# Two token rows and one mirrored block turned by DMA instead of TensorE, in a spectral filter with a gated MLP

## The chip, the core and the metric

The kernel runs on one core of a Trainium2 chip. The metric is the device time of one execution in microseconds (us). A core has a matrix engine (TensorE, PE in the profile; its weight loads are PEld), a vector engine (VectorE, DVE), a scalar engine (ScalarE, ACT), GpSimd (POOL), a queue engine (SyncE, SP), and 16 DMA engines that carry what the queues of SP and ACT issue. [...]

## What is computed

`x` is a 2048 x 512 array in bf16 (2048 tokens). It is normalised per token, and two branches are added to it: a filter in the two-dimensional Fourier domain, and a gated MLP with 1792 hidden columns.

```
xn = layernorm(x)                                   # per token, over 512
X  = rfft2(xn) * (w_r + 1j * w_i)
y  = irfft2(X)                                      # spectral branch
h  = gelu(xn @ w_gate, tanh form) * (xn @ w_up)     # 512 -> 1792
out = x + y + h @ w_down                            # 1792 -> 512
```

## The kernel before

**Tiles.** The tokens form 16 rows of 128 (a row here is 128 tokens on the 128 partitions), four rows to a block. The hidden columns form 14 groups of 128 (`NFC`). For every row the kernel loads `x`, takes mean and variance (`stats`, L519), a reciprocal root (`root_act` L523 for rows 0 and 1, `root_pool` L529 on GpSimd for the others), normalises (`norm`, L535) into `xn`, and turns the 128 x 512 row into `xnT` with features on the partitions. Both branches read `xnT`.

**Turning a row.** There are three ways. `first_half` (L557) turns row 0 in two halves on PE. `turn` (L540) does a row with four PE transposes into PSUM (L550) and one VectorE copy to `xnT` (L555); rows 1, 2 and 3 go this way. `turn_dma` (L577) has SP issue one DMA transpose from SBUF to SBUF; rows 4 to 15 go this way. `mirror(b)` (L589) makes, for each block, one more 128 x 512 tile from the normalised rows (a difference of reversed parts, one VectorE operation) and turns that too: by PE and a VectorE copy (L604, L608) for block 0, by a DMA transpose (L595) for blocks 1 to 3. `fold(b)` (L610) combines `xnT` and the turned mirror tile on VectorE and feeds the first Fourier matmuls (L635, evicted by ScalarE at L640).

**The spectral branch** after that is a long chain of VectorE operations (`tt`, recorded at L467), with small matmuls (L850, L931, L991) and ScalarE evictions between, and ends in additions to `x`, four rows at a time.

**The MLP.** `gated` (L709) does one group for a stretch of tokens: four gate matmuls and four up matmuls (L718) over the four feature parts; each four are a burst, and each burst writes one of three PSUM banks; ScalarE applies gelu to the gate (L723) and copies the up part (L724), VectorE multiplies them into `hT` (L725). A block is 512 tokens wide. Block 0 begins before all its rows are there: `first` (L728) does groups 0 to 2 for rows 0 and 1, row by row; then groups 3 to `NHALF`-1 are done for rows 0 and 1 (256 tokens, first halves); then all groups below `NHALF` for rows 2 and 3 (second halves); then the groups from `NHALF` on for all 512 tokens. Blocks 1 to 3 follow in full width. `down` (L756) sums 14 matmuls (L766) with `wd` for one row; the rows of block b are placed between the groups of block b+1. For the last block, `down` uses PSUM slots of the spectral branch, and VectorE adds straight from PSUM (L777); for the others ScalarE copies (L774) and VectorE adds (L775).

**Loads.** The gate and up weights come in column slabs 0:384 (groups 0 to 2, on ACT's queue), 384:768 (groups 3 to 5), 768:1280 (groups 6 to 9) and 1280:1792 (groups 10 to 13). SP issues, in order: rows 0 to 3 one by one, the slabs 384:768, rows 4 to 7, the slabs 768:1280, rows 8 to 11, the slabs 1280:1792, the Fourier tables (`small`), rows 12 to 15. Each of these is one DMA with a semaphore of its own. `wd` is issued after row 7 is normalised, the table `tf` after row 11, the filter after the last fold.

**The order of work** is set before the program is written out, by a planner (`_Sched`, L145). It simulates the engines with a cost for each operation (for a DMA: bytes at a fixed rate in one queue, plus a lag) and always takes the operation that can start first; among those of the same engine within 0.05 us it takes the one with the smallest key (its ready time plus an offset `key`) or, where one is given, its due time. The result is a fixed order on each engine, with semaphore waits. MLP matmuls carry large, rising keys: they fill PE in their own order wherever no other PE operation is ready. `STAT` and `NORM` are due times: row s (4 and up) has its statistics due at STAT[0] + STAT[1] * (s - 4), its normalisation at NORM[0] + NORM[1] * (s - 4). `gate` is a list of operations after which SP may issue loads that are declared later.

```
filler = []
for fc in range(NFIRST, NHALF):
    filler.append(("g", 0, fc, 0, 256))
for fc in range(NHALF):
    filler.append(("g", 0, fc, 256, 256))
for fc in range(NHALF, NFC):
    filler.append(("g", 0, fc, 0, 512))
```

Of the kernel before, what the change touches and what calls it, by code (L numbers as in the profile page):

```python
# [14 lines left out]
FF = 1792  # L15
P = 128
NFC = 14
NHALF = 6
NFIRST = 3
WARM = 10 * (512,) + (256,)  # L20
HKEY = 1.5
NORM = 15.0, 1.5
STAT = 13.0, 1.2
SLACK = 0.05
MARGIN = 1.0
RATE = 340e3
# [118 lines left out]
class _Sched:  # L145
# [11 lines left out]
    def op(self, eng, cost, fn, reads=(), writes=(), tiles=(), key=0.0, after=(), dma=0, lag=0.0, due=None, land=None):  # L157
        o = _Op()
        o.eng, o.fn, o.cost, o.key, o.dma, o.lag, o.due, o.land = eng, fn, cost, key, dma, lag, due, land
        o.reads, o.writes, o.tiles = reads, writes, [(t, False) for t in tiles]  # L160
        o.extra = [a for a in after if a is not None]
        o.seq = len(self.ops)
        o.end = None
        o.pos = None
        self.ops.append(o)
        return o
# [184 lines left out]
def bass_parallel_sum__spectral_gfnet__glu_gated_geglu__prompt_kernel(  # L351
# [11 lines left out]
    c_small = nc.inline_tensor(small_np, name="c_small")  # L363
# [5 lines left out]
    wgv = B_w_gate.rearrange("(dc p) f -> p dc f", p=P)  # L369
    wuv = B_w_up.rearrange("(dc p) f -> p dc f", p=P)  # L370
# [3 lines left out]
    op = sch.op  # L374

    with ExitStack() as es:
        def sb(name, shape, dt=BF16, cell=0):
            n = int(np.prod(shape))
            t = es.enter_context(nc.sbuf_tensor(name, [P, n], dt))
            return view(t, name, 0, shape, cell)  # L380
# [15 lines left out]
        wg = sb("wg", [4, FF])  # L396
        wu = sb("wu", [4, FF])
        wd = sb("wd", [NFC, D])
        small = sb("smallc", [9, P])
# [21 lines left out]
        ident = small[:, 0]  # L421
# [6 lines left out]
        ps_sp_bf = ps_sp[:, :].bitcast(BF16)  # L428
# [30 lines left out]
        gate = []  # L459

        def dma(q, dst, src, nbytes, wr=None, rd=None, key=0.0, after=(), cost=0.41, lag=0.0, land=None):
            after = tuple(after) + tuple(gate if q == "sp" else ())
            return op(q, cost, lambda e: e.dma_start(dst() if callable(dst) else dst.ap, src() if callable(src) else src.ap),
                      reads=rd if rd is not None else (), writes=wr if wr is not None else (), dma=nbytes, key=key, after=after, lag=lag, land=land)

        def tt(o, a, b, f, n, key=0.0, **kw):
            return op("dve", c_tt(n), lambda e: e.tensor_tensor(o.ap, a.ap, b.ap, f), reads=(a, b), writes=(o,), key=key, **kw)  # L467
# [13 lines left out]
        def load(q, dst, src, nbytes, **kw):  # L481
            return dma(q, dst, lambda: src, nbytes, wr=(dst,), **kw)

        def wload(q, dst, src, lo, hi, **kw):
            return load(q, dst[:, :, lo:hi], src[:, :, lo:hi], (hi - lo) * 1024, **kw)

        k = iter(np.arange(0.0, 1.0, 0.001))
        def rows(lo, hi, land=None):
            return load("sp", x[:, lo:hi], xb[:, lo:hi, :], (hi - lo) * 131072, key=next(k), land=land)
# [8 lines left out]
            rows(i, i + 1, 6.3 + 0.3 * i)  # L498
        for w, v in ((wg, wgv), (wu, wuv)):
            wload("sp", w, v, 384, 768, key=next(k))  # L500
        rows(4, 8)
        for w, v in ((wg, wgv), (wu, wuv)):
            wload("sp", w, v, 768, 1280, key=next(k))
        rows(8, 12)
        for w, v in ((wg, wgv), (wu, wuv)):
            wload("sp", w, v, 1280, FF, key=next(k))
        load("sp", small[:, 1:9].rs([8 * P]), c_small.ap()[:, P:], 262144, key=next(k))
        rows(12, 16)
        op("pool", 0.1, lambda e: e.memset(eps.ap, LN_EPS), writes=(eps,), key=-2)
        op("pool", 0.1, lambda e: e.memset(half.ap, -0.5), writes=(half,), key=0)  # L510

# [4 lines left out]
        def xn(s):  # L516
            return RB(8192 + 512 * (s % 8), [4, P])

        def stats(s, key, due=None, after=()):  # L519
            op("dve", 0.61, lambda e: e.bn_stats(bst[:, s].ap, xs(s).ap), reads=(xs(s),), writes=(bst[:, s],), key=key, due=due, after=after)  # L520
            op("dve", 0.11, lambda e: e.bn_aggr(bag[:, s].ap, bst[:, s].ap), reads=(bst[:, s],), writes=(bag[:, s],), key=key, due=due)
# [7 lines left out]
        def root_pool(s0, n, key):  # L529
            sl = slice(s0, s0 + n)  # L530
            v, y, h = vv[:, sl], rs[:, sl], half[:, sl]
            op("pool", 0.2 + 0.03 * n, lambda e: e.tensor_scalar(v.ap, bag.ap[:, sl, 1], LN_EPS, None, ADD), reads=(bag[:, sl],), writes=(v,), key=key)
            op("pool", 0.5 + 0.14 * n, lambda e: e.tensor_tensor(y.ap, v.ap, h.ap, ALU.pow), reads=(v, h), writes=(y,), key=key)

        def norm(s, key, due=None):  # L535
            o, i = xn(s).rs([512]), xs(s)
            op("dve", 0.34, lambda e: e.tensor_scalar(o.ap, i.ap, bag.ap[:, s, 0:1], rs.ap[:, s:s + 1], SUB, MUL),
               reads=(i, bag[:, s], rs[:, s:s + 1]), writes=(o,), key=key, due=due)

        def turn(s0, n, key):  # L540
            b, sl = s0 // 4, s0 % 4
            t = _T("sp")

            def bank():
                return ps_sp_bf[:, t.slot * 2048:t.slot * 2048 + 512 * n]

            def f(e):
                ins = None
                for i in range(4 * n):
                    ins = e.transpose(bank()[:, i * P:(i + 1) * P], xn(s0 + i // 4).ap[:, i % 4], ident.ap)  # L550
                return ins

            o = xnT[:, b, sl:sl + n].rs([512 * n])
            op("pe", 4 * n * 0.056, f, reads=tuple(xn(s0 + i) for i in range(n)) + (ident,), tiles=(t,), key=-40, lag=0.1)
            op("dve", 0.08 + n * 0.26, lambda e: e.tensor_copy(o.ap, bank()), writes=(o,), tiles=(t,), key=key)  # L555
# [20 lines left out]

        def turn_dma(s):  # L577
            i, o = xn(s), xnT[:, s // 4, s % 4]
            op("sp", 1.25, lambda e: e.dma_start_transpose(o.ap, i.rs([512]).ap), reads=(i,), writes=(o,), dma=425000, key=-5.0)


        Y = R1(0, [16, D])
# [4 lines left out]
        odd, turned = {}, {}  # L587

        def mirror(b):  # L589
            rows = RB(8192 + 2048 * (b % 2), [4, 4, P])  # L590
            g = RB(2048 * (b % 2) + 1024, [4, P])
            odd[b] = RB(2048 * (b % 2) + 1536, [4, P])
            tt(g, rows[:, :, 1, ::-1], rows[:, :, 3, ::-1], SUB, 512, 0.5)
            if b:
                op("sp", 1.25, lambda e: e.dma_start_transpose(odd[b].ap, g.rs([512]).ap), reads=(g,), writes=(odd[b],), dma=425000, key=-5.0)  # L595
                return
            t = _T("sp")

            def bank():
                return ps_sp_bf[:, t.slot * 2048:t.slot * 2048 + 512]  # L600

            def f(e):
                for i in range(4):
                    ins = e.transpose(bank()[:, i * P:(i + 1) * P], g.ap[:, i], ident.ap)  # L604
                return ins

            op("pe", 4 * 0.056, f, reads=(g, ident), tiles=(t,), key=2.0, lag=0.1)
            op("dve", 0.34, lambda e: e.tensor_copy(odd[b].rs([512]).ap, bank()), writes=(odd[b],), tiles=(t,), key=1.0)  # L608

        def fold(b):  # L610
            par = b % 2
# [42 lines left out]
        for s in (2, 3):  # L654
            root_pool(s, 1, -50.0)
            norm(s, -50.0)
            early = sch.ops[-1]
            turn(s, 1, -50.0)
        mirror(0)
        fold(0)  # L660
        for s in range(4, 16):
            stats(s, 0.0, STAT[0] + STAT[1] * (s - 4), (early,))
            if s % 2 == 1:
                root_pool(s - 1, 2, -4.0)
        hold = {}
        for s in range(4, 16):
            norm(s, 0.0, NORM[0] + NORM[1] * (s - 4))
            hold[s] = sch.ops[-1]
            turn_dma(s)
            if s % 4 == 3:  # L670
                mirror(s // 4)
                fold(s // 4)
# [113 lines left out]
# [7 lines that stand above are left out]
# [51 lines left out]
        for v, hh in ((4, (12, 13)), (0, (14, 15)), (2, (8, 9)), (6, (10, 11)), (1, (0, 1)), (7, (4, 6)), (3, (2, 7)), (5, (5, 3))):  # L844
            t = _T("sp")
# [17 lines left out]
        for ri, f in ((0, ADD), (1, SUB)):  # L863
            op("pool", 0.3, lambda e, ri=ri, f=f: e.tensor_tensor(edge.ap[:, ri], ev[0].ap[:, ri], ev[1].ap[:, ri], f),
               reads=(ev[0][:, ri], ev[1][:, ri]), writes=(edge[:, ri],), key=1.0)
# [53 lines left out]
        for i, v in enumerate((0, 4, 1, 7, 2, 6, 3, 5)):  # L919
            t = _T("sp")  # L920

            def f_i(e, v=v, t=t):
# [15 lines left out]
               writes=(gv,), tiles=(t,), key=-0.5)  # L938
# [40 lines left out]
        for jq in range(4):  # L979
# [4 lines left out]
            for jp in (2 * jq, 2 * jq + 1):  # L984
                t = _T("sp")
# [57 lines left out]
```

## Time and profile before

| What | us |
|---|---|
| median of 3 runs | 171.29 (171.24 to 171.5) |
| the profiled execution | 171.29 |
| its span, first to last instruction | 169.4 |
| PE busy | 166.3 |
| VectorE busy | 146.0 |
| ScalarE busy | 106.3 |
| the 12 DMA transposes of rows, issue to landing | 2.5 to 8.4, median 4.5 |

Times inside a profile count from the start of its span. A row of the timeline gives start, duration, engine, line, operation, tiles written <- read, shape and count, and in brackets the idle time before it and what ended it; "SPq" and "ACTq" are instructions that issue DMAs. Matmul durations overlap, so PE's pace is read from starts.

### The profile page before, as it was taken

The numbers are of one execution on the slowest core, as the hardware profiler recorded it, in microseconds if no ns is written. First come the engines' busy times: TensorE is split into PE (matmuls) and PEld (weight loads), VectorE is DVE, ScalarE is ACT, GpSimd is POOL, SyncE is SP. The second block draws the span as 40 slices with busy tenths as digits, with TensorE's granted clock in tenths as the row PEclk, the third lists the DMA queues.
The fourth block names the chain that finished last, engine by engine and source line by source line (L and its number), as shares of the span: only waits on it lengthen the run. The fifth ranks groups of instructions, "written<-read, shape, count | busy, mean of one in ns | idle before, by whom it ended". The sixth has DMA issues, their size and how long they took to land.

```text
span 169.4 us, 2695 instructions
## 1 busy us (share of the span) xinstructions
PE 166.3 (98%) x999; PEld 86.1 (51%) x999; DVE 146.0 (86%) x293; ACT 106.3 (63%) x174; POOL 12.3 (7%) x25
## 2 busy tenths in 40 slices
PE   8999999999999999999999999999999999999994
PEld 3698544445555444444444554644445654444443
DVE  2889999995975999999999999999999869963932
ACT  3588766663979739589663695875738896561000
POOL 2032253500000000020000000000000000000000
PEclk9999999999999999999999999999999999999999
DMA  5999999994025262510000000000000003300322
GB/s 146 338 350 347 286 132 300 224 255 101 0 55 127 76 136 79 159 61 0 0 0 0 0 4 0 0 0 0 4 0 2 0 4 106 128 13 0 124 67 62
DMA packets 22239, 15.62 MB, mean 92 GB/s; under 512 B 9293, under 2 KB 21586, under 8 KB 22226
## 3 DMA queue, kind: packets, MB, share of 16 engines
q1 hardware_dynamic: 21026, 14.63, 34.6%
q10 hardware_dynamic: 1200, 0.82, 1.6%
q8 instruction: 8, 0.13, 0.3%
q14 instruction: 5, 0.04, 0.1%
HBM read 11.38 MB, written 2.10 MB: 80 GB/s over the span
## 4 chain that ended last, share of the span: by engine, by line
PE 98%; DVE 0%; issue 0%
PE ps_gu L718 56%; PE ps_dn L766 21%; PE ps_sp L766 7%; PE ps_dn L476 3%; PE ps_sp L991 2%; PE ps_sp L635 2%; PE ps_sp L850 2%; PE ps_gu L737 1%; PE ps_sp L931 1%; PE ps_sp L932 1%; PE ps_dn L737 1%; PE ps_sp L550 1%; PE ps_sp L854 0%; DVE xnT L575 0%; DVE x_sb L777 0%; PE ps_sp L567 0%
## 5 line engine op out<-in xcount | busy, mean ns | idle before, releaser
L718 PE MATMUL ps_gu<-xnT,wg 128*128 128x512 bf16 (+1 forms) x236 | 56.7, 363 | 0.0
L718 PE MATMUL ps_gu<-xnT,wu 128*128 128x512 bf16 (+1 forms) x236 | 56.7, 363 | 0.0
L723 ACT ACTIVATE gg<-ps_gu 128x512 bf16<-128x512 f32 (+1 forms) x59 | 33.7, 572 | 12.2 <-PE ps_gu L718 8.9
L724 ACT ACTIVATE uu<-ps_gu 128x512 bf16<-128x512 f32 (+1 forms) x59 | 33.9, 575 | 10.5 <-PE ps_gu L718 10.2
L766 PE MATMUL ps_dn<-wd,hT 128*128 128x512 bf16 x168 | 38.9, 379 | 0.0
L467 DVE TENSOR_TENSOR specB<-specB 128x512 bf16<-128x512 bf16 (+2 forms) x58 | 33.6, 611 | 1.9 <-ACT specB L996 1.4
L718 PEld LDWEIGHTS ps_gu<-xnT,wu 128*128 128x128 bf16 x236 | 22.8, 98 | 23.1
L718 PEld LDWEIGHTS ps_gu<-xnT,wg 128*128 128x128 bf16 x236 | 22.6, 98 | 22.0 <-ACT uu L724 0.4
L766 PEld LDWEIGHTS ps_dn<-wd,hT 128*128 128x128 bf16 x168 | 16.3, 98 | 19.1
L725 DVE TENSOR_TENSOR hT<-gg,uu 128x512 bf16<-128x512 bf16 (+1 forms) x59 | 23.1, 395 | 1.8 <-ACT uu L724 1.8
L774 ACT ACTIVATE db<-ps_dn 128x512 bf16<-128x512 f32 x12 | 7.2, 597 | 18.4 <-PE ps_dn L766 18.4
L520 DVE BATCH_NORM_STATS2 bst<-x_sb 128x6 f32<-128x512 bf16 x16 | 10.9, 688 | 3.2 <-DMA x_sb<-in_A_x_dram 3.1
L467 DVE TENSOR_TENSOR specC<-specB 128x1024 bf16<-128x1024 bf16 (+2 forms) x18 | 12.4, 713 | 0.2
L766 PE MATMUL ps_sp<-wd,hT 128*128 128x512 bf16 (+2 forms) x70 | 12.3, 336 | 0.0
L467 DVE TENSOR_TENSOR specB<-specA 128x2048 bf16<-128x2048 bf16 x8 | 9.4, 1219 | 2.7 <-ACT specA L640 2.7
L775 DVE TENSOR_TENSOR x_sb<-db,x_sb 128x512 bf16<-128x512 bf16 x12 | 5.0, 420 | 5.4 <-ACT db L774 5.4
L467 DVE TENSOR_TENSOR specB<-specB,filt 128x2048 bf16<-128x2048 bf16 x8 | 9.4, 1221 | 0.0
L766 PEld LDWEIGHTS ps_sp<-wd,hT 128*128 128x128 bf16 x70 | 6.3, 98 | 6.1 <-DVE x_sb L777 0.2
L859 ACT ACTIVATE specA<-ps_sp 128x1024 bf16<-128x1024 f32 x8 | 7.8, 1035 | 1.3 <-PE ps_sp L850 1.3
L640 ACT ACTIVATE specA<-ps_sp 128x1024 bf16<-128x1024 f32 x8 | 7.7, 1023 | 1.2 <-PE ps_sp L635 1.2
L996 ACT ACTIVATE specB<-ps_sp 128x1024 bf16<-128x1024 f32 x8 | 7.8, 1031 | 0.8 <-PE ps_sp L991 0.8
L937 ACT ACTIVATE specC<-ps_sp 128x1024 bf16<-128x1024 f32 x8 | 7.8, 1039 | 0.0
(71 smaller groups left out, 130.0 us busy)
## 6 DMA issues: line engine op xcount, KB each, us to landing
out_dram<-x_sb SPq DMA_DIRECT2D x15, 128.0 KB, 1.8
wd<-in_B_w_down_dram SPq DMA_DIRECT2D x1, 1792.0 KB, 8.6
x_sb<-in_A_x_dram SPq DMA_DIRECT2D x3, 512.0 KB, 9.2
wg<-in_B_w_gate_dram SPq DMA_DIRECT2D x2, 512.0 KB, 8.6
wu<-in_B_w_up_dram SPq DMA_DIRECT2D x2, 512.0 KB, 9.2
toki<-c_ti SPq DMA_DIRECT2D x1, 768.0 KB, 4.4
tokf<-c_tf SPq DMA_DIRECT2D x1, 576.0 KB, 4.8
x_sb<-in_A_x_dram SPq DMA_DIRECT2D x4, 128.0 KB, 3.5
```

Source lines behind the costliest of these rows:

```text
L467: return op("dve", c_tt(n), lambda e: e.tensor_tensor(o.ap, a.ap, b.ap, f), reads=(a, b), writes=(o,), key=key, **kw)
L520: op("dve", 0.61, lambda e: e.bn_stats(bst[:, s].ap, xs(s).ap), reads=(xs(s),), writes=(bst[:, s],), key=key, due=due, after=after)
L640: op("act", c_act(1024), lambda e, yv=yv, t=t: e.activation(yv.ap, spair(t).rearrange("p (s r i) -> p s i r", s=4, r=4), ACT.Copy), writes ...
L718: ins = e.matmul(gub(t, n), w.ap[:, dc, fc * P:(fc + 1) * P], xnT.ap[:, b, sl, dc, :], start=(dc == 0), stop=(dc == 3))
L723: op("act", c_act(n), lambda e: e.activation(gg.ap[:, gs.slot, 0:n], gub(g, n), ACT.Gelu_apprx_tanh), tiles=(g, gs), key=0.0)
L724: op("act", c_act(n), lambda e: e.activation(uu.ap[:, us.slot, 0:n], gub(u, n), ACT.Copy), tiles=(u, us), key=0.0)
L725: op("dve", c_tt(n), lambda e: e.tensor_tensor(hT.ap[:, h.slot, lo:lo + n], gg.ap[:, gs.slot, 0:n], uu.ap[:, us.slot, 0:n], MUL), tiles=(g ...
L766: ins = e.matmul(bank(), hT.ap[:, hs[(b, fc)].slot, sl * P:(sl + 1) * P], wd.ap[:, fc, lo:lo + n], start=(fc == 0), stop=(fc == NFC - 1))
L774: op("act", c_act(n), lambda e: e.activation(db.ap[:, d.slot, 0:n], bank(), ACT.Copy), tiles=(t, d), key=0.0)
L859: op("act", c_act(1024), lambda e, xv=xv, t=t: e.activation(xv.ap, spair(t), ACT.Copy), writes=(xv,), tiles=(t,), key=-0.5)
L937: op("act", c_act(1024), lambda e, gv=gv, t=t: e.activation(gv.ap, spair(t).rearrange("p (k x i) -> p k x i", k=4, x=4), ACT.Copy), writes ...
L996: op("act", c_act(1024), lambda e, rv=rv, t=t: e.activation(rv.ap, spair(t), ACT.Copy), writes=(rv,), tiles=(t,), key=-0.5)
```

## The change

Rows 2 and 3 (the third and the fourth) and the mirror tile of block 0 are turned by DMA transposes on SP. Groups 3 to 9, not 3 to 5, have first and second halves. The slabs 768:1280 are issued ahead of rows 4 to 7; rows 4 to 7, the slabs 1280:1792, rows 8 to 11, the Fourier tables and rows 12 to 15 are issued after row 3 is normalised and, by their keys, behind the first DMA transposes. The due times for rows 4 to 15 are moved, and the planner counts 0.5 us more for the two new row transposes.

```
-NHALF = 6
+NHALF = 10
...
-NORM = 15.0, 1.5
-STAT = 13.0, 1.2
+NORM = 20.0, 1.5
+STAT = 18.0, 1.5
...
         for w, v in ((wg, wgv), (wu, wuv)):
             wload("sp", w, v, 384, 768, key=next(k))
-        rows(4, 8)
         for w, v in ((wg, wgv), (wu, wuv)):
             wload("sp", w, v, 768, 1280, key=next(k))
-        rows(8, 12)
-        for w, v in ((wg, wgv), (wu, wuv)):
-            wload("sp", w, v, 1280, FF, key=next(k))
-        load("sp", small[:, 1:9].rs([8 * P]), c_small.ap()[:, P:], 262144, key=next(k))
-        rows(12, 16)
...
         def turn_dma(s):
             i, o = xn(s), xnT[:, s // 4, s % 4]
-            op("sp", 1.25, lambda e: e.dma_start_transpose(...), ..., dma=425000, key=-5.0)
+            op("sp", 1.25, lambda e: e.dma_start_transpose(...), ..., dma=425000, key=-5.0, lag=0.5 if s < 4 else 0.0)
...
         def mirror(b):
-            if b:
-                op("sp", 1.25, lambda e: e.dma_start_transpose(odd[b].ap, ...), ..., key=-5.0)
-                return
-            t = _T("sp")
...
-            op("pe", 4 * 0.056, f, reads=(g, ident), tiles=(t,), key=2.0, lag=0.1)
-            op("dve", 0.34, lambda e: e.tensor_copy(odd[b].rs([512]).ap, bank()), ...)
+            op("sp", 1.25, lambda e: e.dma_start_transpose(odd[b].ap, ...), ..., key=-5.0)
...
         for s in (2, 3):
             root_pool(s, 1, -50.0)
             norm(s, -50.0)
             early = sch.ops[-1]
-            turn(s, 1, -50.0)
+            turn_dma(s)
+        gate.append(early)
+        rows(4, 8)
+        for w, v in ((wg, wgv), (wu, wuv)):
+            wload("sp", w, v, 1280, FF, key=next(k))
+        rows(8, 12)
+        load("sp", small[:, 1:9].rs([8 * P]), c_small.ap()[:, P:], 262144, key=next(k))
+        rows(12, 16)
         mirror(0)
         fold(0)
```

More of the change, by code (lines that the diff above doesn't have):

```diff
@@ L578, in turn_dma @@
             i, o = xn(s), xnT[:, s // 4, s % 4]
-            op("sp", 1.25, lambda e: e.dma_start_transpose(o.ap, i.rs([512]).ap), reads=(i,), writes=(o,), dma=425000, key=-5.0)
+            op("sp", 1.25, lambda e: e.dma_start_transpose(o.ap, i.rs([512]).ap), reads=(i,), writes=(o,), dma=425000, key=-5.0, lag=0.5 if s < 4 else 0.0)
         Y = R1(0, [16, D])
@@ L593, in mirror @@
             tt(g, rows[:, :, 1, ::-1], rows[:, :, 3, ::-1], SUB, 512, 0.5)
-            if b:
-                op("sp", 1.25, lambda e: e.dma_start_transpose(odd[b].ap, g.rs([512]).ap), reads=(g,), writes=(odd[b],), dma=425000, key=-5.0)
-                return
-            t = _T("sp")
[L599 to L605, printed above, removed]
-            op("pe", 4 * 0.056, f, reads=(g, ident), tiles=(t,), key=2.0, lag=0.1)
-            op("dve", 0.34, lambda e: e.tensor_copy(odd[b].rs([512]).ap, bank()), writes=(odd[b],), tiles=(t,), key=1.0)
+            op("sp", 1.25, lambda e: e.dma_start_transpose(odd[b].ap, g.rs([512]).ap), reads=(g,), writes=(odd[b],), dma=425000, key=-5.0)
         def fold(b):
```

## The prediction

> **What bounds the kernel now.** I read the page first: its table of busy time and its chain of the work that ended last.
>
> ```profile
> span 169.4 us, 2695 instructions
> ...
> PE 166.3 (98%) x999; PEld 86.1 (51%) x999; DVE 146.0 (86%) x293; ACT 106.3 (63%) x174; POOL 12.3 (7%) x25
> ...
> PE 98%; DVE 0%; issue 0%
> ```
>
> TensorE (PE) is the chain from end to end. So the question at each edit is only: does PE issue less, or does it now wait? I went through PE's starts one by one. From 6.5 us on it starts a 128-column matmul every 0.056 us, a 256-column one every 0.109 and a 512-column one every 0.216, at a granted clock of 1.0, without one pause longer than 0.1 us. Nothing can be gained but instructions taken off PE, and any new pause is paid in full. Then PE's timeline in the stretch that the change touches:
>
> ```profile
> 9.25 0.60 PE L718 MATMUL ps_gu<-xnT,wg 128*128 128x256 bf16 x4
> 9.73 0.60 PE L718 MATMUL ps_gu<-xnT,wu 128*128 128x256 bf16 x4
> 10.16 0.39 PE L550 MATMUL ps_sp<-smallc,specB 128*128 128x128 bf16 x4
> 10.38 0.60 PE L718 MATMUL ps_gu<-xnT,wg 128*128 128x256 bf16 x4
> ...
> 11.26 0.39 PE L550 MATMUL ps_sp<-smallc,specB 128*128 128x128 bf16 x4
> 11.48 0.60 PE L718 MATMUL ps_gu<-xnT,wg 128*128 128x256 bf16 x4
> 11.92 0.39 PE L604 MATMUL ps_sp<-smallc,specB 128*128 128x128 bf16 x4
> 12.14 0.60 PE L718 MATMUL ps_gu<-xnT,wu 128*128 128x256 bf16 x4
> ...
> 17.82 1.03 PE L718 MATMUL ps_gu<-xnT,wg 128*128 128x512 bf16 x4
> ```
>
> The first column is the start. Each transpose burst (L550 twice, L604 once) holds PE for 0.22 us (10.16 to 10.38); the duration column, 0.39, overlaps the next burst. Half-width bursts run to 17.82, full-width ones after. Third, SP's timeline, for what stands in its queue:
>
> ```profile
> 4.53 0.51 SPq L463 DMA_DIRECT2D x_sb<-in_A_x_dram  x1
> 5.08 0.51 SPq L463 DMA_DIRECT2D wg<-in_B_w_gate_dram  x1
> 5.63 1.48 SPq L463 DMA_DIRECT2D wu<-in_B_w_up_dram  x1
> ...
> 16.45 7.36 SPq L579 DMA_TRANSPOSE xnT<-specB  x5
> 23.86 0.58 SPq L463 DMA_DIRECT2D wd<-in_B_w_down_dram  x1
> ```
>
> and the list of DMA issues, asked for one issue at a time, whose last number is the time from issue to landing (rows 4 to 7, then the weight slab 768:1280 of the gate):
>
> ```profile
> x_sb<-in_A_x_dram SPq DMA_DIRECT2D x1, 512.0 KB, 6.6
> ...
> wg<-in_B_w_gate_dram SPq DMA_DIRECT2D x1, 512.0 KB, 7.5
> ```
>
> So the rows land at 11.11, the gate slab at 12.61, and by the same list the up slab at 14.11: the queue serves in order, 512 KB in 1.5 us. Last, VectorE's timeline at the end:
>
> ```profile
> 152.67 0.43 DVE L725 TENSOR_TENSOR hT<-gg,uu 128x512 bf16<-128x512 bf16 x1 [1.30 <-ACT uu L724]
> 155.69 0.42 DVE L775 TENSOR_TENSOR x_sb<-db,x_sb 128x512 bf16<-128x512 bf16 x1 [2.60 <-ACT db L774]
> ...
> 160.00 0.69 DVE L777 TENSOR_TENSOR x_sb<-ps_sp,x_sb 128x512 bf16<-128x512 f32 x1
> ```
>
> There VectorE waits for PE, not PE for VectorE: this is the slack that a later spectral part can use.
>
> **The change part by part.** The base is the profiled execution: 171.29 us, 169.4 of it span and 1.9 outside; it equals the median of the three runs (171.29).
>
> *Taken off PE.* Three bursts of four transposes (rows 2 and 3, the first mirrored block): 3 x 0.22 = **-0.66 us**, all on the path. Three copies on VectorE (0.41 each, 1.2 us) go too; VectorE is not on the path, so 0.
>
> The Trainium skill ("VectorE: DVE Perf Modes", section "The three transpose paths") gives a 128x128 transpose 390 ns on TensorE and 1309 ns by DMA, and its rules advise TensorE wherever PSUM will do, which speaks against this change. By that figure the 12 transposes would be 4.7 us of PE and the sum would end near 167.1; the trace has them at 0.056 us each, and decides.
>
> *Added on PE.* Column groups 6 to 9 of token block 0 are done in two halves. 16 half-width bursts at 0.437 (5.24 us for the 12 from 12.58 to 17.82) stand for 8 full ones at 0.863: 6.99 - 6.91 = **+0.08 us**. ScalarE does 16 evictions at 0.39 for 8 at 0.61, +1.4 us, but 0.39 fits under the 0.437 of a burst. VectorE has 8 products at 0.27 for 4 at 0.42, +0.5 us, less than the copies that went. Both 0.
>
> *A new wait: weights of group 6.* Today groups 6 and up begin at 17.82, after both slabs 768:1280 have landed. After the change PE goes on with first halves of groups 3 to 9. From the rows: group 3's up burst starts at 9.73, and six bursts of 0.437 later, at 12.35, comes group 6's up burst. Rows 4 to 7 no longer stand ahead of the slabs, so each takes the place of the one before it: gate 11.11 (in time for its 11.91), up 12.61. Group 3's up burst started 0.14 after its slab landed (9.59), so group 6's starts at 12.75: **+0.40 us**. Bounds: 0 (a landing by 12.2) and 1.9 (its old landing, 14.11). I take 0.40: the same slot of the queue holds the same bytes. ScalarE frees the PSUM bank for group 4's gate burst only at 10.19, about 0.1 later than PE could use it without the transposes; this lies within the same wait.
>
> *The DMA transposes of rows 2 and 3.* Normalising ends near 9.7 and 10.8. SP then issues row 2, row 3 and the mirrored block at 1.25 us each, to about 13.5; each issue is counted in the shift below. They land behind the up slab: the first transpose behind a load landed 1.3 after it today (22.00, then 23.29), the next 0.5 later. So row 3 lands near 14.4 (bounds: 13.5 by the 2.5 us of an idle queue, 16.0 by the widest step between two transposes, 2.1). PE wants it after first halves of 3 to 9, at 12.75 + 7 x 0.437 = 15.8. Cost 0, at most 0.3. The new second halves are the cover; with 6 groups in halves PE would have waited here.
>
> *Loads moved behind them.* Rows 4 to 7 are issued near 13.5, not 4.53; at 1.5 us per 512 KB they land near 17.5, the slabs 1280: near 19 and 20.5, rows 12 to 15 near 25. Weights of group 10 are wanted at 24.5: 4 us of cover. The new due times put row 7's normalisation at 24.5, 1.4 later if it slips as today (19.5 planned, 20.87 run). Its transpose lands by 28.5 to 31; block 1 begins on PE at 31.45. wd follows at about 28 and lands 8.6 later, 36.6; PE wants it at 38.4. Cost 0, cover 0.5 to 2.
>
> *The spectral part.* The first DMA transpose of the old kind moves from 16.45 to about 20.5, and VectorE has the rest of the row statistics to do from 17.5 instead of 12.2, but with block 0's folding (3.5 us) already behind it. I put the last mirrored block 3.3 us later (46.1 for 42.79), bounds 1 and 6. Of it VectorE can take up 2.1 of idle time before 42.39. From 52.65 to 137.6 VectorE is busy 82.4 of 85 us, so there the delay is passed on whole; at the end it meets the idle time above: 0.3 + 1.3 + 2.6 = 4.2 us. 3.3 is under 4.2: cost 0. The filter loads wait for the last fold and move with it.
>
> Sum: -0.66 + 0.08 + 0.40 = -0.18, **171.1 us**.
>
> **Rivals.** *No wait for the weights* (the slab is early, or the wait smaller than 0.1): -0.58, 170.7. For it: no other load is ahead. Against: 1.5 us per slab is met by every load from 8.45 to 22.00. Chance 0.22. *Spectral part too late, slower*: if the last mirrored block comes more than about 4.2 us late, VectorE finishes after PE's last groups, the last row additions (L777) hold the PSUM slots that the last down projections need, and PE stands still, 1 us for each us beyond. At 6 late: +1.8, 172.9. For it: 3.3 is near 4.2, and VectorE has little rest in between. Against: 2.1 us of earlier idle time not counted. Chance 0.20. *Inputs of block 1 late* (row 7's transpose or wd; 0.5 to 2 us of cover): 171.5 to 172.3. Chance 0.14. *It doesn't do what it says*, the loads slipping ahead of the transposes: the planner gives transposes a key 5 us ahead, so 0. The page's 390 ns, 167: the rows rule it out, 0.
>
> **How the numbers follow.** My forecast has 0.44: 171.1, its own range 170.9 to 171.4. The range runs from 170.6 (no wait) to 172.2, which takes in the late inputs and leaves out most of the late spectral part. A difference under 0.2% (0.34 us) can't be told from none. Faster: 0.22 of the rival and 0.08 of the forecast, where the wait is a little shorter. Same: 0.36. Slower: 0.20 and 0.14.
>
> **What would show it.** Right: no L604 and four L550 matmuls instead of twelve; one pause of about 0.4 us on PE ahead of an L718 up burst near 12.7; none after. VectorE's first 2048-wide spectral addition 1 to 4 us after 52.65, and its idle time near 155 shorter. Wrong: a PE pause near 15.8 (row 3), 31.5 (row 7) or 38.4 (wd), or L777 ahead of PE near 160. A slab that lands by 12.2 makes 170.7; a landing beyond 13 makes it slower than said.

## The result and the profile after

The changed kernel takes 172.16 us (median of 22 runs, 171.37 to 173.13); the kernel before takes 171.53 beside it (22 runs, 171.1 to 173.9). The ratio is 1.0035, 95% interval 1.002 to 1.005: slower, by 0.6 us, where 0.2 us less was forecast. The profiled execution took 172.26 us, 170.2 of it span and 2.06 outside (before: 171.29, 169.4 and 1.87).

These are the same lines of the page as those shown for the kernel before: the size of the program, the busy times and the chain that ended last.

```profile
span 170.2 us, 2739 instructions
...
PE 165.1 (97%) x1007; PEld 88.1 (52%) x1019; DVE 145.8 (86%) x294; ACT 108.0 (63%) x182; POOL 10.4 (6%) x25
...
PE 80%; DVE 9%; DMA 7%; issue 1%; SPq 1%; ACT 0%; DVEq 0%
```

PE is busy 1.2 us less in a span that is 0.8 us longer, and the chain, all PE before, now holds 7% of DMA and 9% of VectorE. (The trace lacks 12 matmul records: 1007 matmuls beside 1019 weight loads. Eleven show as a hole of just one matmul in an even row of starts; the twelfth is the first matmul of the first down projection, which matters below. Busy time has to be read with that in mind.) What PE waited for is in the list of waits, with the total, the number of times and the longest in us:

```profile
PE ps_dn L753 <- DMA wd<-in_B_w_down_dram: 1.1, 1, 1.1
PE ps_dn L476 <- PEq L1015: 0.8, 1, 0.8
PE ps_gu L705 <- DMA wu<-in_B_w_up_dram: 0.2, 1, 0.2
```

L476 is the warm-up at the start. The other two are new: one for the up slab of group 6, and one for `wd`, which the forecast had put at 0. PE's timeline shows both (L705 is the old L718, L753 the old L766), with the weight loads (PEld) that stand ahead of the down projection:

```profile
11.87 0.60 PE L705 MATMUL ps_gu<-xnT,wg 128*128 128x256 bf16 x4
12.68 0.60 PE L705 MATMUL ps_gu<-xnT,wu 128*128 128x256 bf16 x4 [0.21 <-DMA wu<-in_B_w_up_dram]
...
40.01 1.03 PE L705 MATMUL ps_gu<-xnT,wg 128*128 128x512 bf16 x4
41.86 0.11 PEld L753 LDWEIGHTS ps_dn<-wd,hT 128*128 128x128 bf16 x2 [1.32 <-DMA wd<-in_B_w_down_dram]
42.09 1.46 PE L753 MATMUL ps_dn<-wd,hT 128*128 128x512 bf16 x6 [1.06 <-DMA wd<-in_B_w_down_dram]
```

Starts give the true loss. A half burst from 11.87 ends its turn at 12.31, and the next starts at 12.68, so 0.37 us. For `wd` the missing record has to be put back: two weight loads, one for each matmul, stand ahead of the matmul at 42.09, and a matmul of 512 columns takes 0.216, so the down projection began at 41.87. A full burst of four from 40.01 ends its turn at 40.87, so the pause is 1.00. (The brackets differ: the modelled end of a matmul overlaps the next, and the second bracket also holds the missing matmul.) Why `wd` is late stands in SP's timeline:

```profile
9.58 2.61 SPq L573 DMA_TRANSPOSE xnT<-specB  x2
12.23 1.26 SPq L588 DMA_TRANSPOSE specB<-specB  x1
13.54 0.58 SPq L463 DMA_DIRECT2D x_sb<-in_A_x_dram  x1
...
26.06 3.47 SPq L573 DMA_TRANSPOSE xnT<-specB  x2
29.57 1.26 SPq L588 DMA_TRANSPOSE specB<-specB  x1
30.88 2.57 SPq L573 DMA_TRANSPOSE xnT<-specB  x2
33.50 0.58 SPq L463 DMA_DIRECT2D wd<-in_B_w_down_dram  x1
```

The first three lines are rows 2, 3, the first mirror tile and rows 4 to 7, issued where the forecast put them. The row at 26.06 is the transposes of rows 6 and 7. Row 7's is issued at 28.26, but `wd`, which waits only for row 7 to be normalised, is issued at 33.50: the second mirror tile (29.57) and rows 8 and 9 (30.88, two issues) stand between. It lands 8.3 us later, at 41.82, and PE begins with it 0.05 after that.

Account of PE, from its starts, after less before (pauses of all kinds above 0.012 us counted): transposes off -0.66, halves +0.08, pauses up to 26 us +0.46 (0.50 for 0.04; besides the 0.37 there is one of 0.10 ahead of group 3's up burst at 9.66), the pause for `wd` +1.00, later pauses +0.02; the first half burst starts 0.13 earlier (9.12 for 9.25). Sum +0.77; the last matmul starts 0.76 later (167.69 for 166.93), and the span is 0.8 longer. The rest of the profiled difference of 0.97 is the time outside the span, +0.19.

**My theory (W)**: the loss is the wait for `wd`, and it comes from `wd`'s place in SP's queue, not from its bytes. **Rival T**: the later spectral part holds PE at the end, too. **Rival D**: the DMA transposes cost by themselves. T already has this against it in VectorE's timeline at the end:

```profile
59.27 2.36 DVE L467 TENSOR_TENSOR specB<-specA 128x2048 bf16<-128x2048 bf16 x2 [2.27 <-ACT specA L620]
...
161.87 0.69 DVE L764 TENSOR_TENSOR x_sb<-ps_sp,x_sb 128x512 bf16<-128x512 f32 x1 [0.42 <-PE ps_sp L753]
```

The first 2048-wide addition comes 6.6 us later than before (52.65), far more than forecast, but at 161.87 VectorE still waits for PE.

### The profile page after: what moved, and what is told of

It reads as the page before. It is cut to its first block, busy times and chain, and to the rows that moved or that the text cites. A ratio compares the mean times of both kernels' runs of the same rounds, so it can differ in the third digit from the quotient of the medians.

```text
span 170.2 us, 2739 instructions
## 1 busy us (share of the span) xinstructions
PE 165.1 (97%) x1007; PEld 88.1 (52%) x1019; DVE 145.8 (86%) x294; ACT 108.0 (63%) x182; POOL 10.4 (6%) x25
## 4 chain that ended last, share of the span: by engine, by line
PE 80%; DVE 9%; DMA 7%; issue 1%; SPq 1%; ACT 0%; DVEq 0%
PE ps_gu L705 39%; PE ps_dn L753 21%; PE ps_sp L753 7%; DMA wd<-in_B_w_down_dram 5%; DVE bst L514 4%; PE ps_dn L476 3%; DMA x_sb<-in_A_x_dram 3%; PE ps_sp L615 2%; PE ps_sp L978 2%; DVE hT L712 2%; PE ps_sp L837 2%; DVE specB L531 1%; PE ps_gu L724 1%; PE ps_sp L918 1%; PE ps_sp L919 1%
## 5 line engine op out<-in xcount | busy, mean ns | idle before, releaser
L705 PE MATMUL ps_gu<-xnT,wu 128*128 128x512 bf16 (+1 forms) x252 | 57.4, 350 | 0.2 <-DMA wu<-in_B_w_up_dram 0.2
L705 PE MATMUL ps_gu<-xnT,wg 128*128 128x512 bf16 (+1 forms) x252 | 57.4, 350 | 0.0
L711 ACT ACTIVATE uu<-ps_gu 128x512 bf16<-128x512 f32 (+1 forms) x63 | 34.6, 549 | 11.6 <-PE ps_gu L705 11.0
L710 ACT ACTIVATE gg<-ps_gu 128x512 bf16<-128x512 f32 (+1 forms) x63 | 34.5, 548 | 11.4 <-PE ps_gu L705 10.2
L753 PE MATMUL ps_dn<-wd,hT 128*128 128x512 bf16 x157 | 37.2, 379 | 1.6 <-DMA wd<-in_B_w_down_dram 1.1
L705 PEld LDWEIGHTS ps_gu<-xnT,wu 128*128 128x128 bf16 x252 | 24.3, 98 | 22.2 <-ACT uu L711 0.5
L705 PEld LDWEIGHTS ps_gu<-xnT,wg 128*128 128x128 bf16 x252 | 24.2, 98 | 21.0
L712 DVE TENSOR_TENSOR hT<-gg,uu 128x512 bf16<-128x512 bf16 (+1 forms) x63 | 23.8, 384 | 3.6 <-ACT uu L711 3.1
L753 PEld LDWEIGHTS ps_dn<-wd,hT 128*128 128x128 bf16 x168 | 16.0, 98 | 19.7 <-DMA wd<-in_B_w_down_dram 1.3
L753 PE MATMUL ps_sp<-wd,hT 128*128 128x512 bf16 (+2 forms) x69 | 12.2, 336 | 0.1
L753 PEld LDWEIGHTS ps_sp<-wd,hT 128*128 128x128 bf16 x70 | 6.3, 98 | 6.1 <-DVE x_sb L764 0.2
```

The source lines that it names most:

```text
L705: ins = e.matmul(gub(t, n), w.ap[:, dc, fc * P:(fc + 1) * P], xnT.ap[:, b, sl, dc, :], start=(dc == 0), stop=(dc == 3))
L710: op("act", c_act(n), lambda e: e.activation(gg.ap[:, gs.slot, 0:n], gub(g, n), ACT.Gelu_apprx_tanh), tiles=(g, gs), key=0.0)
L711: op("act", c_act(n), lambda e: e.activation(uu.ap[:, us.slot, 0:n], gub(u, n), ACT.Copy), tiles=(u, us), key=0.0)
L712: op("dve", c_tt(n), lambda e: e.tensor_tensor(hT.ap[:, h.slot, lo:lo + n], gg.ap[:, gs.slot, 0:n], uu.ap[:, us.slot, 0:n], MUL), tiles=(g ...
L753: ins = e.matmul(bank(), hT.ap[:, hs[(b, fc)].slot, sl * P:(sl + 1) * P], wd.ap[:, fc, lo:lo + n], start=(fc == 0), stop=(fc == NFC - 1))
```

## The experiments

Each ratio is to the kernel before on the same chip: its median is 171.37 us beside kernels one to four, 171.51 beside five to eight and 171.43 beside nine to eleven.

**One (e1): `wd` ahead in the queue.** The changed kernel, with one key:

```
-        load("sp", wd, wdv, NFC * 131072, key=next(k), after=(hold[7],))
+        load("sp", wd, wdv, NFC * 131072, key=-4.9, after=(hold[7],))
```

> One key is changed: wd is issued right behind row 7's transpose instead of behind the transposes of block 1's mirrored tile, row 8 and row 9. Theory W (the late wd is what made the changed kernel slower: 1.2 us of wait at the first down projection in its profile, some 0.8 on the median): wd lands near 38, PE has no wait near 41, the profiled execution takes 171.0 to 171.2, the median about 0.8 less than the changed kernel, ratio to before about 0.999. Rival T (the spectral part, 6.3 us later, would hold the end by itself at about 161.4 in L764): PE's wait near 41 goes but another comes near 161, the gain is 0.3 at most, ratio to before 1.001 to 1.003.

171.59 us, ratio 1.0016 (1.0001 to 1.0031). Its timelines of SP and PE, with PE's weight loads:

```profile
29.48 0.58 SPq L463 DMA_DIRECT2D wd<-in_B_w_down_dram  x1
```

```profile
37.75 1.03 PE L705 MATMUL ps_gu<-xnT,wu 128*128 128x512 bf16 x4
38.40 0.53 PEld L753 LDWEIGHTS ps_dn<-wd,hT 128*128 128x128 bf16 x3
38.83 1.03 PE L753 MATMUL ps_dn<-wd,hT 128*128 128x512 bf16 x4
```

`wd` goes out 4.0 us earlier and lands at 37.57, and the first down projection follows its burst without a pause. (Its first matmul, due when the burst's turn ends at 38.61, is a missing record here too; its weights load at 38.40.) From the first half burst to the last matmul PE takes 157.72 us, where the changed kernel takes 158.57 and the kernel before 157.67. Not all of the 1.00 comes back: the planner orders the work anew, and a pause of 0.31 appears at 23.93, where ScalarE's gelu wants an output slot whose VectorE product stands behind two fold operations. The ratio falls from 1.0035 to 1.0016, but the two intervals overlap, so it is the trace that shows the repair. No pause at the end: T is out, although the ratio lies in T's range and above the 0.999 of W.

**Two (e2): smaller slabs.** The changed kernel, with the slabs 768:1280 in two parts, so that group 6's weights land first:

```
-        for w, v in ((wg, wgv), (wu, wuv)):
-            wload("sp", w, v, 768, 1280, key=next(k))
+        for lo, hi in ((768, 1024), (1024, 1280)):
+            for w, v in ((wg, wgv), (wu, wuv)):
+                wload("sp", w, v, lo, hi, key=next(k))
```

> Both slabs 768:1280 are loaded as 768:1024 (gate, up), then 1024:1280 (gate, up); wd is left late. If the wait of 0.38 us at group 6's up burst is due to the order of the slabs alone, it goes (the up slab of groups 6 and 7 lands near 11.1, wanted at 12.3). Theory W: the wait for wd takes up what PE gained (PE then stands at the first down projection 0.4 earlier, and wd is not earlier), so the time stays within 0.2 us of the changed kernel, ratio to before 1.002 to 1.005. Rival (the early wait is paid in full): 0.4 us less than the changed kernel, ratio 1.001.

171.80 us, ratio 1.0028 (1.0016 to 1.0041). The pause at group 6 is gone; pauses of 0.27 (at 9.38, for group 3's up slab; 0.10 in the changed kernel) and 0.26 (at 15.32, for row 3, whose transpose landed at 15.60 and not at 13.45) take its place, and `wd` (landed at 41.60) still holds PE for 0.83. So this wait was real, but removing it alone uncovers the next input.

**Three (e3): both edits together.**

```
+        for lo, hi in ((768, 1024), (1024, 1280)):
...
+        load("sp", wd, wdv, NFC * 131072, key=-4.9, after=(hold[7],))
```

> Both edits: wd right behind row 7's transpose, slabs 768:1280 split. Theory W: neither wait is left, the sum is that of the prediction without its waits, -0.66 + 0.08 = -0.6 us against before, 170.7 in the profile, ratio to before 0.9965. Rival T: the end is held by the spectral part, and the ratio stays above 0.999.

171.33 us, ratio 0.9999 (0.9988 to 1.001): level with the kernel before, not 0.35% under it. That is the ratio of Rival T, but PE waits for nothing at the end here either. In its profile PE pauses 0.46 us in all (0.23 before), and from the first half burst to the last matmul it takes 157.33 us for 157.67: -0.34, just what -0.66 + 0.08 + 0.24 of pauses makes. So PE's part of the sum is right; in the mean of its runs the span is 0.23 shorter than before (169.34 for 169.57), and the time outside the span is 0.19 longer (2.02 for 1.83), which takes it back.

**Four (e4): no added DMA transpose.** The changed kernel, with rows 2, 3 and the first mirror tile turned by PE as before; loads, halves and due times stay changed:

```
-            turn_dma(s)
+            turn(s, 1, -50.0)
```

(and in `mirror`, the removed PE branch for block 0 back).

> The changed kernel with rows 2, 3 and the first mirrored tile turned by PE as before; loads, halves and due times as changed. Theory W: PE has its 0.66 us of transposes back, the wait at group 6 shrinks to nothing as PE comes there 0.4 to 0.7 later, the loads are issued some 2 us earlier and wd stands behind two transposes only, so its wait is under 0.3: 171.3 to 171.7, ratio 1.000 to 1.002. Rival D (the three added DMA transposes cost time of their own in SP's queue, and the loads' new place is harmless): wd lands in time by 2 us or more and the ratio is 1.000.

171.99 us, ratio 1.0035 (1.0022 to 1.0048): as slow as the changed kernel, without one of its added DMA transposes, and above W's 171.3 to 171.7. Its pauses are 0.08 up to 26 us, 0.38 for `wd` (landed 39.85) and 0.58 later (0.19 before). So D is out as it stands: without the added transposes `wd` is still late, and moved loads, halves and due times bring a loss with them. But the transposes add to it: with them `wd` lands 2.0 us later (41.82), and all pauses together come to 1.71 us in the changed kernel for 1.04 here. What they take off PE, 0.66, is there as pauses instead.

**Five (f1): halves and slabs alone.** The kernel before, with ten halves and rows 4 to 7 behind the slabs 768:1280:

```
-NHALF = 6
+NHALF = 10
...
-        rows(4, 8)
         for w, v in ((wg, wgv), (wu, wuv)):
             wload("sp", w, v, 768, 1280, key=next(k))
+        rows(4, 8)
```

> The kernel before with ten groups in halves and the slabs 768:1280 ahead of rows 4 to 7; transposes on PE, all other loads, due times as before. The changed kernel and the four variants so far spend 2.0 us outside their span, the kernel before 1.83. Theory H (the halves bring this: 32 more matmuls and their weight loads, 8 more evictions, 4 more products than before): time outside the span 2.0, span +0.1 to +0.2, time +0.25 to +0.4, ratio 1.0015 to 1.0025. Rival L (the loads held back behind row 3 bring it): 1.83 outside, span +0.1, ratio 1.0005. In both wd lands near 33 to 34 and PE does not wait for it.

177.91 us, ratio 1.037 (1.0334 to 1.0405). Neither theory had this. Its waits:

```profile
PE ps_gu L718 <- ACT gg L723: 3.5, 4, 1.2
...
PE ps_dn L766 <- DMA wd<-in_B_w_down_dram: 2.3, 1, 2.3
```

PE waits for ScalarE, and ScalarE's gelu for VectorE's products (8.3 us in all), which stand behind row statistics, normalisations and fold operations in the same stretch. Rows 4 to 7 land at 14.16 here, not 11.11, so this kernel doesn't tell the halves from the later rows. `wd` lands at 35.86, not at 33 to 34, and PE does wait for it.

**Six (f2): the mirror tile alone.** The kernel before, with only the first mirror tile by DMA (in `mirror`, the diff's hunk alone).

> The kernel before with one part of the change alone: the first mirrored tile by a DMA transpose, which the planner puts behind rows 12 to 15 and ahead of row 4's transpose. PE loses 4 transposes (0.22 us), all other work stays. If the first fold has time until 28 us as in the kernel before (its last two operations start at 28.4), the time falls by 0.22, ratio 0.9987. Rival: VectorE, in its fixed order, stands at the first fold until the tile lands near 23.5, the products queue behind it, PE waits 0.5 or more: ratio 1.002 or more.

171.53 us, ratio 0.9996 (0.998 to 1.0012). No new pause; from the first half burst to the last matmul PE takes 157.44 us for 157.67, which is the 0.22 expected. The profiled span is 169.1 for 169.4, and 2.2 us lie outside it. For the time it stays undecided: the expected 0.9987 lies inside the interval, and so does no change.

**Seven (f3): the old due times.** Kernel three, with

```
-NORM = 20.0, 1.5
-STAT = 18.0, 1.5
+NORM = 15.0, 1.5
+STAT = 13.0, 1.2
```

> The fastest variant so far (wd behind row 7, slabs 768:1280 split) with the due times of before (statistics from 13.0 at 1.2, normalising from 15.0 at 1.5). If the due times are not what made the changed kernel slower, the time stays within 0.15 us of that variant, ratio 0.999 to 1.0008. Rival: the later due times delay row 7 and the spectral part, wd lands 1 us earlier with the old ones and the small waits of the half-width stage go: 0.2 us or more faster.

178.69 us, ratio 1.0391 (1.0346 to 1.0435), in neither expectation. PE pauses 6.2 us in all, 5.4 of it in three waits for ScalarE (4.9 by the list of waits). From that list and ScalarE's timeline:

```profile
PE ps_gu L706 <- ACT gg L711: 4.9, 3, 1.9
```

```profile
22.23 0.38 ACT L711 ACTIVATE gg<-ps_gu 128x256 bf16<-128x256 f32 x1 [2.28 <-DVE hT L713]
```

From 18.55 to 21.85 VectorE does four row statistics and two normalisations; the products wait, ScalarE stands 2.28 us for a free `gg` slot, and PE for ScalarE. Another 1.7 us is no pause. After the third of these waits PE runs at half its pace:

```profile
30.00 1.91 PE L706 MATMUL ps_gu<-xnT,wg 128*128 128x512 bf16 x4
31.71 1.87 PE L706 MATMUL ps_gu<-xnT,wu 128*128 128x512 bf16 x4
33.41 1.03 PE L706 MATMUL ps_gu<-xnT,wg 128*128 128x512 bf16 x4
```

A full burst takes 1.71 us from 30.00 and again from 31.71, where 0.863 is usual, and the granted clock from 30.0 to 33.4 is 0.50. The runs of this kernel go with it: 176.91 us in the one at a mean clock of 1.0, 178.10 and 178.18 at 0.99, 179.19 and more at 0.981. What lowers the clock was not tried. A half-width product is due every 0.87 us and there are four slots, so halves pass on a stretch that full width (a product every 1.73 us) would bridge; that last is argued from these figures, no run has full width there. The later due times, the only difference from three, are therefore a condition of the ten halves.

**Eight (f4): six halves again.** The changed kernel, with

```
-NHALF = 10
+NHALF = 6
```

> The changed kernel with six groups in halves as before. PE has done the first halves of groups 3 to 5 at 9.12 + 6 x 0.437 = 11.75, row 3's transpose lands at 13.5: if the ten halves are the cover for the DMA transposes, PE waits 1.8 us there, none at group 6; wd is late as in the changed kernel, but PE comes to it 1.4 later, so that wait goes. 172.0 to 172.6, ratio 1.003 to 1.007. Rival (the ten halves are not needed): no wait beyond 0.3 and a ratio of 1.001 or less.

175.39 us, ratio 1.0221 (1.0184 to 1.0258). Its waits and the pause for row 3:

```profile
PE ps_dn L753 <- DMA wd<-in_B_w_down_dram: 1.8, 1, 1.8
PE ps_gu L705 <- DMA xnT<-specB: 1.5, 1, 1.5
```

```profile
13.64 0.61 PE L705 MATMUL ps_gu<-xnT,wg 128*128 128x256 bf16 x4 [1.53 <-DMA xnT<-specB]
```

By starts PE stands 1.70 us for row 3 (1.8 expected) and 1.75 for `wd`, which was not expected: it lands at 41.31, near its 41.82 in the changed kernel, and is wanted at 39.61. So the four more halves do cover rows 2 and 3, as the prediction's step has it. The two pauses make the profiled span 172.2; the median lies a further microsecond off, because 2.1 to 3.5 us of these runs lie outside the span.

**Nine to eleven (g1, g2, g3): the time outside the span.** It is 1.83 to 1.85 in the mean for the kernel before and about 2.0 for the changed one and kernels one to four. In the traces with 2.0 an 8 KB load of instructions follows after the last instruction. *Theory C*: three more VectorE instructions bring that load, and with it 0.2 us. Nine is the kernel before with three one-element memsets on VectorE at the start:

```
+        for i in range(3):
+            op("dve", 0.06, lambda e, i=i: e.memset(pad.ap[:, i:i + 1], 0.0), writes=(pad[:, i:i + 1],), key=-99.0)
```

> The kernel before with three extra one-element memsets on VectorE at the very start, where it is idle until 3 us; nothing else differs. In the traces so far every kernel with 315 or more instructions on VectorE's queue (the changed kernel, its four first variants, the halves alone) has an 8 KB instruction load after the end of its span and 2.0 to 2.2 us outside the span; the kernel before has 313, no such load and 1.83. Theory C (the load of one more block of instructions at the end costs about 0.2 us): 316 instructions, a load after the end, 2.0 outside, span unchanged, ratio 1.001. Rival (the time outside depends on something else): 1.83 outside, ratio 1.000.

171.43 us, ratio 1.0004 (0.9993 to 1.0015). The load comes, and 2.05 us lie outside, but the span is 0.1 to 0.2 shorter: no time is lost. Ten is kernel three, with four tiny VectorE operations moved to GpSimd:

```
-            tiny(xb_[:, :, 1, 0:1], t1[:, 1, :, 0:1], t2[:, 0, :, 0:1], SUB)
+            tiny(xb_[:, :, 1, 0:1], t1[:, 1, :, 0:1], t2[:, 0, :, 0:1], SUB, q="pool")
```

(and the same for column 256).

> The variant with wd behind row 7 and split slabs, with four small edge operations moved from VectorE to GpSimd, so that VectorE's queue has about 311 instructions. Theory C: no instruction load after the end, 1.8 us outside the span, span as that variant (169.3), time 171.1 to 171.2 where the kernel before has 171.4: ratio 0.9985. Rival: 2.0 outside, ratio 1.000.

171.80 us, ratio 1.0058 (1.0024 to 1.0093), in two groups, seven runs at 171.3 to 171.9 and five at 173.3 to 173.8, which is not explained. The load is gone, and 2.12 us still lie outside the span, as 2.16 do in kernel six, whose trace has no such load either: C falls. Eleven is kernel three with rows 2, 3 and the mirror tile on PE, by the same edit as four, so that the DMA transposes are the only difference between it and three.

> The variant with wd behind row 7 and split slabs, with rows 2, 3 and the first mirrored tile turned by PE again. It measures the 12 transposes alone, with no late wd to hide them: PE has 0.66 us more. If neither has waits, the span is 0.6 to 0.7 above that variant's 169.3, ratio 1.003 to 1.004. Rival (the DMA transposes cost elsewhere what they save): the span rises by less than 0.3.

171.52 us, ratio 1.0012 (0.9996 to 1.0028). Against kernel three the mean span is 0.4 longer (169.72 for 169.34); in the profiles the last matmul starts 0.44 later, and 0.64 counted from the first half burst (9.04 here, 9.24 there). Both profiles have 0.46 us of pauses, so that 0.64 is the 0.66 taken off PE, once the inputs are in time; the burst row starts 0.20 earlier here, and the span shows 0.4 where 0.6 to 0.7 was expected. The ratios alone don't tell the two kernels apart, since their intervals overlap.

## Why the prediction was wrong

*The step that failed*: "wd follows at about 28 and lands 8.6 later, 36.6; PE wants it at 38.4. Cost 0, cover 0.5 to 2." The 8.6 was right (8.3). The issue was not: I took `wd` as next behind row 7's transpose, though the transposes' key ("5 us ahead"), which I used myself against another rival, also puts the second mirror tile and rows 8 and 9 ahead of a load that carries a plain rising key. Three issues at 1.31 from one to the next are 3.9 us. The other 1.6 us came before them: for `wd` at 28, row 7's transpose had to go out at 26.7; the row was normalised by 26.35, but its transpose stood behind row 6's issue of 2.16 and went out at 28.26. So 33.50, not 28. The trace of the kernel before had the sign of it: the five transposes from 16.45 that stand ahead of `wd` there are rows 4 to 7 and row 8. PE's need moved too, to 40.87, since the planner put three more full-width bursts first, so the wait that I had put at 0 cost 1.00. What happened is the rival "Inputs of block 1 late", 171.5 to 172.3, to which I had given 0.14. Experiment one confirms the step: with that key alone changed, the trace has no wait there.

*Taken off PE, -0.66, and halves, +0.08*: right. The account of three closes to 0.01 with them, and eleven against three shows 0.64. The 390 ns of the Trainium skill ("VectorE: DVE Perf Modes", section "The three transpose paths") would have made the removal worth 4.7 us, an estimate from that figure; the runs bear out 0.056 us per transpose in this stream. Its 1309 ns for a DMA transpose is near the 1.26 us that SP takes here to issue one of four blocks, but that is a different quantity; from issue to landing row 7 took 2.5.

*Weights of group 6, +0.40*: right, 0.37. The slabs landed at 11.03 and 12.54 (11.11 and 12.61 forecast). Group 3's up slab, which was not in the sum, cost 0.10, since PE came to it 0.13 earlier. That every load from 8.45 to 22.00 meets 1.5 us per slab was a misreading: rows 8 to 11 landed 2.7 after the slab ahead of them (16.84 after 14.11).

*Rows 2 and 3*: cost 0, right. Row 3 landed at 13.45 (14.4 forecast, lower bound 13.5, 15.8 wanted); eight shows the 1.7 us that the added halves cover.

*Loads moved behind them, group 10 and row 7*: cost 0, right. The slabs 1280:1792 landed at 19.86 and 21.66 (19 and 20.5 forecast), row 7's transpose at 30.75 (28.5 to 31); PE waited for neither.

*Spectral part*: cost 0, right, but its size was wrong. The last mirror tile landed 6.4 us later (49.16 for 42.79; forecast 3.3, upper bound 6), and the last spectral sums began 6.3 later (143.92 for 137.58). By my rule that 4.2 us can be taken up, 2 us of loss would have followed. None did (the changed kernel and three have no pause at the end). The 4.2 of idle time was right: from the last sums to the row additions VectorE is busy 16.7 of 16.8 us (143.92 to 160.76), before 18.0 of 22.4 (137.58 to 160.00). What I left out is other VectorE work, products of the MLP above all: 1.3 us of it now stands ahead of the sums. The last 0.8 us is the lateness of PE, with which the row additions begin.

*ScalarE and VectorE, "both 0"*: true of this change, but under a condition I did not name. Seven shows 5.4 us of pauses on PE and 1.7 us more at half the clock, and five 3.5 us of pauses, where row statistics fall between the products of the ten halves.

*1.9 outside the span*: 2.03 in the mean. This is not explained. Between kernels it goes from 1.8 (seven) to 2.2 (six) and 2.7 (eight); nine shows 0.2 more of it without 0.2 more time, so I don't book it as a loss of the change, and for three it stays open whether the missing 0.2 us lies there.

No kernel here beats the kernel before by more than its interval; three is level with it.

## What to carry to other kernels

Where one engine is the whole chain and a change takes only 0.66 us off it, write down for every transfer that moves what the queue will hold ahead of it (by the keys of the order, not by the order of the source) and when it is wanted; a cover of 0.5 to 2 us is no cover when one more queue item costs 1.3. Removing one late input shows the next, so test the repairs together as well as alone. Before a pause is read from starts, count matmuls against weight loads: one missing record of this kernel looks like 0.2 us of waiting. Narrower tiles halve the time that each slot can bridge: look at what the evicting and the multiplying engine have due in that stretch before putting their cost at nothing.

## What was not expected of the hardware

The gap between two DMA transposes that SP issued back to back was mostly 0.4 to 0.6 us at landing, but sometimes 2.0: rows 2 and 3 landed at 13.01 and 13.45 in the changed kernel, at 13.56 and 15.60 in two and at 13.47 and 15.48 in three. It is 2.0 in all four traces with split slabs in which these rows go by DMA (two, three, seven and ten). Behind the 1.8 MB load of `wd`, the issue of one DMA transpose took 2.89 us on SP instead of 1.26 (at 34.12 in the changed kernel). In seven the granted clock fell to 0.50 for 3.4 us after PE had stood three times for 1.3 to 2.1 us within 9 us; in the profiles of five and eight, pauses of up to 2.2 us left it at 1.0. The cause of none of these was tried.
